# An eighth pair of attention chunks shares its weights, two copies and a read change engine, and some tiles move by 128 bytes

## The chip, the cores and the metric

The kernel runs on one core of a Trainium2 chip. The metric is the device time of one execution in microseconds (us). The engines are TensorE (PE, with its weight loads as PEld), VectorE (DVE), ScalarE (ACT), GpSimd (POOL) and SyncE (SP, which here only issues transfers).

## The reference

Two stages. The first is an attention without softmax over 8 batches of 2496 rows, whose weights are the squared positive part of the scaled scores and whose result is multiplied by `u`. The second is a mixture of experts on the 19968 rows that come out.

```python
scores = (1.0 / S) * (z @ z.T)          # z: 2496 x 64 in each batch
attn = np.maximum(scores, 0.0) ** 2
x = u * (attn @ v)                      # u, v: 2496 x 256

do_compute = x @ w_skip > 0             # rows that go to an expert
logits = x @ w_gate                     # 8 experts
e = argmax(logits); gate = softmax(logits)[e]
out = x + gate * (relu(x @ w1[e]) @ w2[e])   # 256 -> 1024 -> 256
```

The scores of a batch are symmetric: the weights of keys A for queries B are those of keys B for queries A, transposed.

## The kernel before

**Chunks and steps.** The queries of a batch are cut into five chunks, c0 to c4 (four of 512 rows, c4 of 448). The keys are cut into ten pairs of 128-row blocks, p = 0 to 9, and keys p belong to the rows of chunk p // 2. A chunk is ten steps, one for each p, in the order of the table `ORDER` (the first chunk of the first batch goes 0 to 9), so the attention has 400 steps. In a step, PE does 24 matmuls into the four accumulators of the chunk (`attend`, 18 where p = 9): first 12 for the half d = 0 of the 256 columns, then 12 for d = 1. The accumulators of a half are called `acc[0]` and `acc[1]` (two row groups of PE, of 64 rows each, work side by side, each into its own), and the sum of both is the result.

**Weights.** The weights of a step are made two steps ahead (`stage(s + 2)`, called ahead of the step's own matmuls). `weights` has two ways. A plain tile is computed: six score matmuls on PE (`scores`, L251) into one of two PSUM buffers, Relu (L290) and Square (L291) on ACT. A recalled tile comes from DRAM (`recall`, L280, issued three steps earlier still). Then both are split into a high part `ah` (L310, on ACT or DVE by `on_act`) and a rest `al` (L314, DVE).

**Pairs.** For each pair (A, B) in `PAIRS` chunk A keeps its weights for the keys of B: DVE transposes them (`keep`, L268, two of each tile), SP writes them to DRAM, and chunk B, later in the same batch, recalls the two tiles for the keys of A and computes no scores for them. Batch 0 has no pairs with chunk 0. `EXTRA` names plain tiles whose `ah` is cast on ACT, beside all tiles of pairs.

**End of a chunk.** After its last step (`finish`), each accumulator is read from PSUM: `part(d, 1)` copies `acc[1]` of half d to SBUF (L366), `part(d, 0)` adds `acc[0]` to it (DVE, L368). Then come a product with `u` (L371), transposes of the rows (L375) and stores. In emission order `part(0, ...)` comes between the two halves of the last step, `part(1, ...)` after the second. The next chunk's accumulators take the same four PSUM buffers, in the order in which the pool gets them back.

**Routing.** After every second chunk the list `after` sets, by steps after the chunk's end, the logits' matmuls (`gates`, L406, +2), their transposes from PSUM (`logits`, L428 to L432, +3), the routing on DVE (+4), the gate's Exp (+5) and `place` (+6), which counts tokens by matmuls with a triangle and with ones (L476) and reads the counts from PSUM on DVE (L480, L482). Both PSUM tiles, named `psm`, take one of the two buffers that the scores use.

**Experts.** From about 1330 us on, 40 units of up to three 128-token tiles run through the 8 experts: `unit` multiplies the turned tokens `xt` with the first weights (L593) and the hidden values with the second (L612). `xt` shares its buffers with `rt` of the attention. The tile `shift` (L527) is used by nothing; it moves the tiles that are allocated behind it.

**Order.** Each engine works through its own list in program order: an instruction that waits holds up all behind it on that engine.

Of the kernel before, what the change touches and what calls it, by code (L numbers as in the profile page):

```python
# [8 lines left out]
F32 = mybir.dt.float32  # L9
# [4 lines left out]
ALU = mybir.AluOpType  # L14
AX = mybir.AxisListType
PSUM = bass.MemoryType.PSUM

P = 128
# [7 lines left out]

PAIRS = ((0, 1), (0, 2), (1, 2), (1, 3), (2, 3), (2, 4), (3, 4))
ORDER = (  # L30
# [5 lines left out]
)  # L36
EXTRA = ((8,), (3, 8), (4, 5), (1,), ())


C_TRI, C_REV, C_OFF, C_IDS, C_THR, C_END = 0, 128, 192, 256, 260, 270  # L40
# [2 lines left out]
def f32(ap):  # L43
    return ap.bitcast(F32)
# [3 lines left out]
def attn_moe(ctx, tc, zT, uT, v, wg, w1, w2, cst, pad, out):  # L48
# [4 lines left out]
    nc = tc.nc  # L53
# [5 lines left out]
    E = w1.shape[0]  # L59
# [15 lines left out]
    rp = ctx.enter_context(tc.tile_pool(name="rp", bufs=2))  # L75
    gp = ctx.enter_context(tc.tile_pool(name="gp", bufs=1))
    op = ctx.enter_context(tc.tile_pool(name="op", bufs=2))
# [139 lines left out]
    def pairs(b):  # L217

        return PAIRS if b else [x for x in PAIRS if x[0]]

# [4 lines left out]
    def on_act(ci, p):  # L225
        b, c = ci // NQ, ci % NQ
        j = p // 2
        if (b, c) == (0, 0):
            return p in (4, 6)
        return (j, c) in pairs(b) or (c, j) in pairs(b) or p in EXTRA[c]  # L230

    kept = {x: dram.tile([QC, QC], F32, name="kept%d%d" % x) for x in PAIRS}
    HALF = (slice(0, 64), slice(64, 128))
# [109 lines left out]
    def spare(rows64=True):  # L343

        if rows64:
            return ps_s.tile([P, 2, QC], F32, name="psm", tag="s")
        return ps_acc.tile([P, 1, QC], F32, name="psm", tag="acc")
# [3 lines left out]
    def finish(ci):  # L351

        b, q0, n = chunks[ci]
        t0 = b * S + q0
        xT = xTs[ci] = uts.pop(ci)

        nm = n // 32
        xrow = xp.tile([P, QC // 32, D // 4], F32, name="xrow", tag="xrow")


        e = xrow.rearrange("p a b -> p (a b)").rearrange("p (d q) -> p d q", d=2)

        def part(d, t, acc):

            if t:
                (nc.scalar.copy if d else nc.vector.tensor_copy)(e[:, d, :n], acc[1][:, :n])  # L366
            else:
                nc.vector.tensor_add(e[:, d, :n], acc[0][:, :n], e[:, d, :n])  # L368

        def mul():  # L370
            nc.vector.tensor_mul(xT[:, :, :n], e[:, :, :n], xT[:, :, :n])  # L371

        def turn_rows(d):

            nc.vector.transpose(  # L375
                xrow[:, :nm, 32 * d : 32 * d + 32], xT[:, d, :n].rearrange("p (m i) -> p m i", i=32)
            )

        dsts = [xr, out]

        def store():
            dst = dsts.pop(0)
            for a in range(4):
                nc.sync.dma_start(
                    dst[t0 : t0 + n, 64 * a : 64 * a + 64].rearrange("(m i) e -> i m e", i=32),
                    xrow[32 * a : 32 * a + 32, :nm, :],
                )

        return part, mul, lambda: turn_rows(0), lambda: turn_rows(1), store

    def routing(cis, rows64=True):

        K = 4 * len(cis)
# [19 lines left out]
        pair = rp.tile([P, 8, 2], I32, name="pair", tag="pair", bufs=3)  # L413
        dest = rp.tile([P, 8], I32, name="dest", tag="dest", bufs=3)

        ex = rp.tile([P, 8, E], F32, name="ex", tag="ex")[:, :K, :]
        sm = rp.tile([P, 8, 1], F32, name="sm", tag="sm")[:, :K, :]
# [45 lines left out]
            nc.scalar.activation(ex, dls[0], AF.Exp)  # L463

        def place():
            nc.vector.tensor_reduce(sm, ex, axis=AX.X, op=ALU.add)
            nc.vector.tensor_scalar_add(sm, sm, 1e-9)
            nc.vector.reciprocal(f32(pair[:, :K, 1:2]), sm)
            ps = spare(rows64)
            hot_, pre_ = (x.rearrange("p t e -> p (t e)") for x in (hot, pre))  # L470
            ds_ = rp.tile([P, 8, E], F32, name="ds_", tag="ds_")[:, :K, :]
            df = rp.tile([P, 8], F32, name="df", tag="df")[:, :K]
            halves = list(enumerate(HALF)) if rows64 else [(0, slice(0, P))]
            for w, x in ((tri, hot_), (ones, pre_)):
                for t, h in halves:
                    nc.tensor.matmul(  # L476
                        ps[:, t, : K * E], w[h, :], x[h, :], start=(w is tri), stop=(w is ones)
                    )
            c = ps[:, :, : K * E].rearrange("p k (t e) -> p k t e", e=E)
            nc.vector.tensor_add(ds_, c[:, 0], eoff[:, :K, :])  # L480
            if rows64:
                nc.vector.tensor_add(ds_, c[:, 1], ds_)  # L482
            nc.vector.tensor_mul(ds_, ds_, hot)
            nc.vector.tensor_reduce(df, ds_, axis=AX.X, op=ALU.add)
            put_sums.append(df)
# [3 lines left out]
        def put_in(t0, t1):  # L489
# [4 lines left out]
            for t in range(t0, t1):  # L494
# [10 lines left out]
                puts.append(put)  # L505

        return gates, logits, route, counts, gate, place, put_in

    def count(name, rows64=True):
# [14 lines left out]
        for k in range(n):  # L524
            xgs[t].append(zp.tile([P, 2, D], F32, name="xg" + t, tag="z" + "hl"[k % 2], bufs=ZBUFS))

    gp.tile([P, 40], F32, name="shift")  # L527
    xtf, xts = [], [[], []]

    def x_tiles():  # L530
# [139 lines left out]
    def stage(s):  # L670
        if s < len(steps):
            aa[s] = weights(*steps[s], old.pop(s, None))
            return aa[s][2:]
        return lambda: None, lambda: None

    def put_some():

        for _ in range(4):
            if puts and puts[0][0] < step[0] - 1:
                _, dst, src = puts.pop(0)  # L680
                nc.sync.dma_start(dst, src)

    def ahead(s):
        if s < len(steps):
            ci, p = steps[s]
            if (p // 2, ci % NQ) in pairs(ci // NQ):
                old[s] = recall(ci, p)
                known.add(s)
# [62 lines left out]
    for s, (ci, p) in enumerate(steps):  # L751
        b, q0, n = chunks[ci]
        k = s % NP
        step[0] = s
        ahead(s + LA + 3)
        high, low = stage(s + LA)
        if k == 0:
            accs[ci] = [[ps_acc.tile([P, QC], F32, name="acc", tag="acc") for _ in range(2)] for _ in range(2)]
        ah, al = aa.pop(s)[:2]
        if k < NP - 1:  # L760
            high()
            low()
            for d in range(2):
                attend(b, n, p, d, accs[ci][d], ah, al, k == 0, False)
        else:
            part, mul, rows0, rows1, store = finish(ci)
            acc = accs.pop(ci)
            if s + LA in known:

                high()  # L770
                low()
                high = low = lambda: None
            for d in range(2):
                attend(b, n, p, d, acc[d], ah, al, False, True)
                part(d, 1, acc[d])
                if d:
                    high()
                part(d, 0, acc[d])
            low()
            mul()  # L780

            new.append(ci)
            if ci < NC - 1:
                after = [(rows0, 2), (rows1, 3), (store, 4), (store, 5)]
                if ci % 2 == 0:
                    gates, logits, route, counts, gate, place, put_in = routing(new)
                    after = [(gates, 2), (rows0, 2), (logits, 3), (rows1, 3), (route, 4), (counts, 4),
                             (store, 4), (gate, 5), (store, 5), (place, 6)]
                    for t in range(0, 4 * len(new), 2):
                        f = lambda put_in=put_in, t=t: put_in(t, t + 2)  # L790
                        if s + 6 + t < len(steps):
                            after.append((f, 6 + t))
                        else:
                            left.append(f)
                    new = []
                for f, k in after:
                    todo.setdefault(s + k, []).append(f)
            else:
                gates, logits, route, counts, gate, place, put_in = routing(new, False)
        for f in todo.pop(s, []):  # L800
            f()
        put_some()
# [55 lines left out]
    for e in range(E):  # L858
# [3 lines left out]
        for i in range(NFIX):  # L862
# [24 lines left out]
            if i == NFIX - 1:  # L887

                add(fills, (5, lambda: turn_pe(pair(e, NFIX + 1), turned(e, NFIX), 1, 2 * P)))
                n = nc.values_load(fin["arm"][0:1, e : e + 1], min_val=0, max_val=narms - 1)  # L890
# [6 lines left out]
        for arm in tc.Switch(n, narms, hint="rest%d" % e):  # L897
# [9 lines left out]
            for j, w in enumerate(ws):  # L907
                i = NFIX + j
                fills = {}
                after = ws[j + 1 :]  # L910
# [73 lines left out]
```

## Time and profile before

| what | value |
|---|---|
| median of three runs | 1842.22 us (1838.9 to 1843.4) |
| the profiled execution | 1840.9 us |
| its span | 1839.1 us |
| PE busy over the span | 1797.2 us (98%) |
| DVE, ACT busy | 1226.3 us (67%), 1117.7 us (61%) |
| attention | about 0 to 1330 us |
| experts | about 1330 to 1839 us |

The busy times say which engine is the bound; where an engine sat idle, and whose work ended that, is read from the waits and the timelines of the places in question.

### The profile page before, as it was taken

Reading aid. Unit: us, or ns where it says so; the run is one execution under the profiler, and the core shown is the slowest. Engines: PE = TensorE matmul, PEld = TensorE weight load, DVE = VectorE, ACT = ScalarE, POOL = GpSimd, SP = SyncE. Lnnn points to the kernel's source line nnn. Section 1 sums busy time; section 2 is a strip of 40 time slices with the busy share of each in tenths; the row PEclk is TensorE's granted clock in tenths of the full one; section 3 lists DMA queues with packets and bytes.
Section 4 is the critical chain, followed back from the end, with each engine's and each line's share of the span. In section 5 each row is a group of like instructions: output and inputs, shape, how many; then the busy total and the mean of one; then the engine's idle time right before and its main releaser. Section 6 shows DMA issues by size and latency. Waiting matters only on the chain. (4 is left out here: it accounts for less than half of the span.)

```text
span 1839.1 us, 40432 instructions
## 1 busy us (share of the span) xinstructions
PE 1797.2 (98%) x15928; PEld 1616.5 (88%) x15928; DVE 1226.3 (67%) x2169; ACT 1117.7 (61%) x1414; POOL 433.4 (24%) x429
## 2 busy tenths in 40 slices
PE   8999999999999999999999999999899999999998
PEld 6888888978888898788999888888799999999998
DVE  7777787877877787788778777868653343334432
ACT  8876776777677677767776776777433223323321
POOL 0001101210120220111022011112254556535621
PEclk9999999999999999999999999999999999999999
DMA  5574587477648746874683686468452233313210
GB/s 184 127 190 126 134 212 181 106 182 184 156 113 202 190 104 166 202 174 115 166 206 96 162 224 154 106 174 197 118 118 67 78 96 106 83 51 101 82 40 26
DMA packets 384501, 252.77 MB, mean 137 GB/s; under 512 B 204515, under 2 KB 318437, under 8 KB 384176
## 3 DMA queue, kind: packets, MB, share of 16 engines
q1 hardware_dynamic: 370176, 225.79, 49.5%
q0 software_dynamic: 13712, 22.99, 4.5%
q8 instruction: 141, 2.31, 0.5%
q14 instruction: 184, 1.51, 0.3%
q10 hardware_dynamic: 288, 0.17, 0.0%
HBM read 138.46 MB, written 111.05 MB: 136 GB/s over the span
## 5 line engine op out<-in xcount | busy, mean ns | idle before, releaser
L338 PE MATMUL acc<-ah,vh 64*128 64x512 f32 (+1 forms) x3120 | 722.5, 386 | 9.6 <-DVE xrow L366 4.9
L338 PE MATMUL acc<-ah,vl 64*128 64x512 f32 (+1 forms) x3120 | 707.1, 384 | 0.0
L314 DVE TENSOR_TENSOR al<-r,ah 128x1024 fp32r<-128x1024 f32 (+3 forms) x464 | 478.9, 1048 | 191.5 <-ACT ah L310 179.4
L338 PE MATMUL acc<-al,vh 64*128 64x512 f32 (+1 forms) x3120 | 554.8, 384 | 0.1
L338 PEld LDWEIGHTS acc<-ah,vh 64*128 64x128 f32 x3120 | 418.2, 184 | 64.9 <-DVE xrow L368 11.7
L338 PEld LDWEIGHTS acc<-ah,vl 64*128 64x128 f32 x3120 | 418.0, 185 | 38.7
L290 ACT ACTIVATE r<-ps 128x1024 f32<-128x1024 f32 (+1 forms) x292 | 294.8, 1010 | 255.7 <-PE ps L251 224.2
L495 POOL DMA_INDIRECT lst<-pair,dest x160 | 184.5, 1153 | 1105.4 <-DVE dest L493 1006.1
L338 PEld LDWEIGHTS acc<-al,vh 64*128 64x128 f32 x3120 | 363.0, 184 | 41.8 <-DVE al L314 2.6
L310 ACT CAST ah<-r 128x1024 fp32r<-128x1024 f32 (+1 forms) x329 | 277.0, 871 | 59.9 <-DMA r<-kept 34.7
L291 ACT ACTIVATE r<-r 128x1024 f32<-128x1024 f32 (+1 forms) x292 | 304.8, 1044 | 9.2
L598 ACT ACTIVATE hh<-psh 128x512 fp32r<-128x512 f32 (+1 forms) x172 | 99.0, 584 | 299.7 <-PE psh L593 259.8
L612 PE MATMUL y<-w2t,hh 128*128 128x256 f32 x1328 | 246.3, 286 | 0.4 <-ACT hh L598 0.4
L593 PE MATMUL psh<-xt,w1h 128*128 128x256 f32 (+1 forms) x1280 | 235.3, 284 | 1.9 <-ACT xt L566 1.5
L612 PEld LDWEIGHTS y<-w2t,hh 128*128 128x128 f32 x1328 | 208.2, 192 | 0.7 <-ACT hh L598 0.7
L599 DVE SCALAR_TENSOR_TENSOR hl<-psh,hh 128x512 fp32r<-128x512 f32 (+1 forms) x172 | 113.3, 671 | 136.4 <-ACT hh L598 131.2
L593 PEld LDWEIGHTS psh<-xt,w1h 128*128 128x128 f32 x1280 | 197.3, 188 | 3.0 <-issue 2.5
L612 PE MATMUL y<-w2t,hl 128*128 128x256 f32 x664 | 188.7, 284 | 0.3 <-DVE hl L599 0.2
L593 PE MATMUL psh<-xt,w1l 128*128 128x256 f32 (+1 forms) x640 | 181.1, 283 | 0.0
L251 PE MATMUL ps<-zh 64*128 64x512 f32 (+1 forms) x584 | 144.8, 407 | 14.4 <-ACT zh L108 4.6
L251 PE MATMUL ps<-zl,zh 64*128 64x512 f32 (+1 forms) x584 | 140.4, 391 | 0.0
L268 DVE STREAM_TRANSPOSE rt<-r 128x512 f32<-128x512 f32 x216 | 140.2, 687 | 0.0
(170 smaller groups left out, 1703.9 us busy)
## 6 DMA issues: line engine op xcount, KB each, us to landing
kept<-rt SPq DMA_DIRECT2D x216, 256.0 KB, 5.2
r<-kept SPq DMA_DIRECT2D x432, 128.0 KB, 3.9
raw<-in_v SPq DMA_DIRECT2D x80, 256.0 KB, 3.7
ut<-in_uT SPq DMA_DIRECT2D x32, 512.0 KB, 5.2
xr<-xrow SPq DMA_DIRECT2D x128, 128.0 KB, 3.2
out<-xrow SPq DMA_DIRECT2D x128, 128.0 KB, 3.2
raw<-in_w SPq DMA_DIRECT2D x64, 256.0 KB, 3.6
zf<-in_zT SPq DMA_DIRECT2D x40, 256.0 KB, 3.7
```

What stands on the lines that cost most here:

```text
L251: nc.tensor.matmul(to, k[h, o : o + P], queries(q, h, n), start=(m == 0), stop=(m == 2))
L268: nc.vector.transpose(t[:, :, 32 * k : 32 * k + 32], r[:, x, :].rearrange("p (m i) -> p m i", i=32))
L290: nc.scalar.activation(r[:, :, :n], ps[:, :, :n], AF.Relu, scale=isc)
L291: nc.scalar.activation(r[:, :, :n], r[:, :, :n], AF.Square)
L310: (nc.scalar.copy if on_act(ci, p) else nc.vector.tensor_copy)(h_, r_)
L314: nc.vector.tensor_sub(l_, r_, f32(h_))
L338: nc.tensor.matmul(acc[t][:, :n], w[h, x, dd], a[h, x, :n], start=(first and t not in halves[:m]), stop=(last and t not in halves[m + 1 :]),)
L495: put = nc.gpsimd.indirect_dma_start(out=lst, out_offset=bass.IndirectOffsetOnAxis(ap=dest[:, t : t + 1], axis=0), in_=pair[:, t, :], in_o ...
L593: nc.tensor.matmul(ps[:, j * W : (j + 1) * W], wt[:, a, o : o + P], x[:, d, :W], start=(m == 0), stop=(m == 5),)
L598: nc.scalar.activation(hh[:, : G * W], ps[:, : G * W], AF.Relu)
L599: nc.vector.scalar_tensor_tensor(hl[:, : G * W], ps[:, : G * W], 0.0, f32(hh[:, : G * W]), op0=ALU.max, op1=ALU.subtract)
L612: nc.tensor.matmul(ys[t], h[:, tt], w2t[f][:, k, :], start=(f == 0 and m == 0 and t % 2 == 0), stop=(f == NF - 1 and m == 2), skip_group_c ...
```

## The change

1. The pair (0, 3) joins `PAIRS`: in batches 1 to 7 chunk 0 keeps its tiles for the keys 6 and 7 too, and chunk 3 recalls its tiles for the keys 0 and 1.
2. `ORDER` gets other rows for c0 to c3; `EXTRA` puts the casts of c3's p = 6 and 7 (plain tiles) and of c4's p = 1 and 3 on ACT.
3. The copy of half 0's `acc[1]` at a chunk's end moves from DVE to ACT, where that of half 1 already is.
4. `place` copies the counts from PSUM to a new SBUF tile `c` on ACT, and DVE reads them there; the sum and reciprocal of the gate come after the copy in the program.
5. `logits` comes two steps after the chunk's end, not three, behind `gates` and ahead of `rows0`.
6. `shift` shrinks from 40 to 8 floats. With `c` (512 bytes) ahead of them, the tiles behind it end up at other offsets: `xt` from 206240 and 214432 to 206624 and 214816, so that their address within 512 bytes goes from 416 to 288.

```diff
-PAIRS = ((0, 1), (0, 2), (1, 2), (1, 3), (2, 3), (2, 4), (3, 4))
+PAIRS = ((0, 1), (0, 2), (0, 3), (1, 2), (1, 3), (2, 3), (2, 4), (3, 4))
 ORDER = (
-    (0, 1, 6, 2, 3, 7, 4, 8, 5, 9),
-    (2, 0, 3, 1, 4, 5, 8, 6, 7, 9),
-    (0, 4, 1, 6, 2, 7, 3, 8, 9, 5),
-    (2, 0, 3, 1, 8, 4, 9, 5, 6, 7),
+    (0, 1, 2, 3, 8, 4, 5, 6, 7, 9),
+    (2, 3, 0, 4, 1, 5, 8, 6, 7, 9),
+    (4, 0, 1, 6, 2, 7, 3, 8, 9, 5),
+    (6, 0, 2, 1, 8, 3, 9, 4, 5, 7),
     (0, 1, 2, 3, 4, 5, 6, 7, 8, 9),
 )
-EXTRA = ((8,), (3, 8), (4, 5), (1,), ())
+EXTRA = ((8,), (3, 8), (4, 5), (6, 7), (1, 3))
...
             if t:
-                (nc.scalar.copy if d else nc.vector.tensor_copy)(e[:, d, :n], acc[1][:, :n])
+                nc.scalar.copy(e[:, d, :n], acc[1][:, :n])
...
         def place():
-            nc.vector.tensor_reduce(sm, ex, axis=AX.X, op=ALU.add)
-            nc.vector.tensor_scalar_add(sm, sm, 1e-9)
-            nc.vector.reciprocal(f32(pair[:, :K, 1:2]), sm)
             ps = spare(rows64)
...
-            c = ps[:, :, : K * E].rearrange("p k (t e) -> p k t e", e=E)
+
+            c = rp.tile([P, 2, 8, E], F32, name="c", tag="c", bufs=1)[:, : len(halves), :K, :]
+            nc.scalar.copy(c.rearrange("p k t e -> p k (t e)"), ps[:, : len(halves), : K * E])
+            nc.vector.tensor_reduce(sm, ex, axis=AX.X, op=ALU.add)
+            nc.vector.tensor_scalar_add(sm, sm, 1e-9)
+            nc.vector.reciprocal(f32(pair[:, :K, 1:2]), sm)
             nc.vector.tensor_add(ds_, c[:, 0], eoff[:, :K, :])
...
-    gp.tile([P, 40], F32, name="shift")
+    gp.tile([P, 8], F32, name="shift")
...
-                    after = [(gates, 2), (rows0, 2), (logits, 3), (rows1, 3), (route, 4), (counts, 4),
+                    after = [(gates, 2), (logits, 2), (rows0, 2), (rows1, 3), (route, 4), (counts, 4),
                              (store, 4), (gate, 5), (store, 5), (place, 6)]
```

The first place is ACT's list around the end of c0 in batch 5. Before:

```order
L290 ACTIVATE r<-ps 128x1024
L291 ACTIVATE r<-r 128x1024
L310 CAST ah<-r 128x1024
L366 COPY xrow<-acc 128x512
L290 ACTIVATE r<-ps 128x1024
L291 ACTIVATE r<-r 128x1024
```

In the changed kernel the same place reads:

```order
L290 ACTIVATE r<-ps 128x1024
L291 ACTIVATE r<-r 128x1024
L290 ACTIVATE r<-ps 128x1024
L291 ACTIVATE r<-r 128x1024
L366 COPY xrow<-acc 128x512 x2
L310 CAST ah<-r 128x1024 x2
```

One copy has become two, and right ahead of them stands the Relu and Square of c1's second step, which is now a plain tile, where the cast of a recalled one stood.

The second place is DVE's list at the `place` of one pair of chunks (`ds_`, `df` and `dest` are the slots in the experts' lists). Before:

```order
L314 TENSOR_TENSOR al<-r,ah 128x1024
L466 TENSOR_REDUCE sm<-ex 128x8
L467 TENSOR_SCALAR sm<-sm 128x8
L468 RECIPROCAL pair<-sm 128x8
L480 TENSOR_TENSOR ds__7403<-psm,cs 128x64
L482 TENSOR_TENSOR ds__7403<-psm,ds__7403 128x64
L483 TENSOR_TENSOR ds__7403<-ds__7403,hot 128x64
```

In the changed kernel:

```order
L479 TENSOR_REDUCE sm<-ex 128x8
L480 TENSOR_SCALAR sm<-sm 128x8
L481 RECIPROCAL pair<-sm 128x8
L482 TENSOR_TENSOR ds__7418<-c,cs 128x64
L484 TENSOR_TENSOR ds__7418<-c,ds__7418 128x64
L485 TENSOR_TENSOR ds__7418<-ds__7418,hot 128x64
```

DVE's own order is the same; what it reads is now `c` and not `psm`. The reader of `psm` is on ACT's list, between the cast of one tile and the Relu of the next:

```order
L463 ACTIVATE ex<-dl 128x64
L290 ACTIVATE r<-ps 128x1024
L291 ACTIVATE r<-r 128x1024
L310 CAST ah<-r 128x1024
L478 COPY c<-psm 128x128
L290 ACTIVATE r<-ps 128x1024
```

The copy of the counts is the only instruction that has been added there.

One thing does not show in these lists. In the program as built, the second accumulator that a new chunk writes (`acc[1]` of half 0) stands in the PSUM buffer of the old chunk's half 0 `acc[0]` before the change (released by the add L368; at the end of c0 it is that of half 1's `acc[1]`, released by ACT's copy). After the change it stands at every boundary in the buffer of the old chunk's half 1 `acc[1]`, released by ACT's second copy. The first accumulator stands in the buffer of half 0's `acc[1]` before and after.

## Rows read from the trace of the kernel before

**Rows 1.** Window of the attention: length; PE, PEld, DVE, ACT, POOL busy; clock, DMA share, GB/s.

```profile
0.00:1330.00 1330.00, 1301.79 (x11825) 1123.34 (x11826) 1027.51 (x1775) 963.79 (x1108) 185.29 (x175) 1.00 0.65 161
```

**Rows 2.** Waits of PE's matmuls: total us, times, longest.

```profile
PE acc L338 <- DVE xrow L366: 4.9, 7, 1.3
...
PE acc L338 <- DVE xrow L368: 3.5, 14, 0.6
...
PE ps L251 <- DVE ds__6468 L482: 1.8, 1, 1.8
...
PE ps L251 <- DVE lg L428: 1.1, 3, 0.4
PE ps L251 <- DVE lg L432: 0.9, 4, 0.2
...
PE ps L251 <- DVE ds__18482 L482: 0.2, 1, 0.2
```

**Rows 3.** Timeline, end of c0 in batch 5: start, length, instruction [idle before].

```profile
866.71 0.41 PE L251 MATMUL ps<-zh 64*128 64x512 f32 x2
...
866.93 0.59 ACT L366 COPY xrow<-acc 128x512 f32<-128x512 f32 x1 [1.44 <-DMA ut<-in_uT]
...
867.18 0.42 PE L251 MATMUL ps<-zh,zl 64*128 64x512 f32 x2
867.36 0.68 DVE L366 COPY xrow<-acc 128x512 f32<-128x512 f32 x1
...
868.10 0.51 PE L338 MATMUL acc<-ah,vh 64*128 64x512 f32 x2 [0.50 <-DVE xrow L366]
...
868.44 0.39 PE L338 MATMUL acc<-ah,vl 64*128 64x512 f32 x2
```

**Rows 4.** The same view for PE's weight loads.

```profile
PEld acc L338 <- DVE xrow L368: 11.7, 23, 0.9
...
PEld acc L338 <- DVE xrow L366: 9.7, 14, 1.7
```

**Rows 5.** Timeline at a place in batch 2.

```profile
461.43 0.39 PE L338 MATMUL acc<-al,vh 64*128 64x512 f32 x2
...
463.59 0.50 PE L251 MATMUL ps<-zh 64*128 64x512 f32 x2 [1.77 <-DVE ds__6468 L482]
```

**Rows 6.** A group of the page: count, busy us, mean ns, idle before.

```profile
L268 DVE STREAM_TRANSPOSE rt<-r 128x512 f32<-128x512 f32 x216 | 140.2, 687 | 0.0
```

**Rows 7.** Timeline at the end of batch 4 (c4 to c0).

```profile
828.29 0.40 PE L251 MATMUL ps<-zh 64*128 64x512 f32 x2
...
829.20 1.03 ACT L290 ACTIVATE r<-ps 128x1024 f32<-128x1024 f32 x1 [0.50 <-PE ps L251]
...
831.23 0.52 ACT L366 COPY xrow<-acc 128x448 f32<-128x448 f32 x1
831.29 0.40 PE L251 MATMUL ps<-zh,zl 64*128 64x512 f32 x2
```

**Rows 8.** ACT's groups in the attention: count, busy us, mean ns, idle before.

```profile
L291 ACT ACTIVATE r<-r 128x1024 f32<-128x1024 f32 x244 | 259.0, 1062 | 7.7
...
L310 ACT CAST ah<-r 128x1024 fp32r<-128x1024 f32 x233 | 241.4, 1050 | 36.5 <-DMA r<-kept 27.9 <-PE acc L338 2.0 <-DVE ut L371 1.2
...
L366 ACT COPY xrow<-acc 128x512 f32<-128x512 f32 x32 | 18.8, 588 | 18.5 <-PE acc L338 11.8 <-DMA r<-kept 4.3 <-DMA ut<-in_uT 2.2
```

**Rows 9.** Timeline of two experts' units: first matmuls, each row a run.

```profile
1432.82 0.39 PE L593 MATMUL psh<-xt,w1h 128*128 128x256 f32 x2
...
1437.58 0.39 PE L593 MATMUL psh<-xt,w1h 128*128 128x256 f32 x2
...
1444.52 0.40 PE L593 MATMUL psh<-xt,w1h 128*128 128x256 f32 x2
...
1449.47 0.40 PE L593 MATMUL psh<-xt,w1h 128*128 128x256 f32 x2
```

**Rows 10.** Waits of ACT: total us, times, longest.

```profile
ACT ah L310 <- DMA r<-kept: 34.7, 25, 2.2
```

## The prediction

> **What bounds the kernel now.** I read the page's busy times first: PE is busy for 1797.2 of 1839.1 us. The window over the attention says that this holds there too: 1301.8 of 1330 us, with the granted clock at 1.00, the upper of its two levels (2.4 GHz) [rows 1]. DVE and ACT are busy for 77% and 72% of the attention, the transfers for 65%. So a part of the change is worth only what it takes from PE: matmuls that vanish, or idle time of PE that vanishes or appears. Next I read what PE waited for. Three kinds of waits recur in the attention [rows 2]: the accumulators at a chunk's end (L366 and L368, 21 waits, 8.4 us), the counts of `place` (L482, six waits from 1.8 down to 0.2; the four not shown are 1.8, 1.8, 1.5 and 0.6, 7.7 us together) and the turned logits (L428 and L432, 7 waits, 2.0 us). Last come the timelines of one place and of two chunk ends, to see what stands ahead of the late instruction. I cost the change against the profiled execution, 1840.9 us, which lies 1.3 us under the median of 1842.2.
>
> **How much a wait really costs.** The idle time printed with a matmul is less than what PE lost. In the timeline of a chunk end [rows 3] the pairs of matmuls start every 0.23 us (866.71, then 867.18 two pairs later), so the pair after 867.18 was due at 867.41. It came at 868.10, 0.69 late, and the next one came after 0.34 and not 0.23, another 0.11: 0.80 us for a printed 0.50, 0.3 more. The weight loads count 37 such waits (23 and 14) with 21.4 us [rows 4], which is an upper bound, since they run ahead of the matmuls. With 0.3 for each of the 37 on top of the matmuls' 8.4, the chunk ends cost 19.5 us now, between bounds of 8.4 and 21.4. At a `place` the next pair was due at 461.43 + 0.23 = 461.66 and came at 463.59 [rows 5]: 1.93, next to a printed 1.77, so I add 0.2 for each of the six and get 8.9. For the logits I add 0.3 for each of seven: 4.1 (at least 2.0).
>
> **Part 1, scores that vanish.** In seven batches chunk 3 recalls two tiles more, so 14 tiles of scores go. A tile is three pairs of matmuls, 3 x 0.23 = 0.70 us [rows 3]. All of it is on PE's path: -9.8 us. What replaces it lies beside PE: 28 more transposes on DVE at 0.687 us (19 us) [rows 6], against 40 copies that leave DVE (below); 14 fewer pairs of Relu and Square on ACT (2.1 us each, -29 us) [rows 7, 8]. The transfers of 28 writes and 56 reads more ride on queues whose share is 0.65 [rows 1]. I cost them at nothing for PE, as long as the recalled tiles land in time (rival 2).
>
> **Part 2, the place.** The PSUM tile of the counts is released today by DVE's second read, which stands behind an `al` and three small operations in DVE's list. Afterwards ACT reads it, right behind the cast that is due in that step, and by the built program the next scores go to the other of the two buffers in every batch; the buffer of the counts is wanted only one step, over 2.7 us, later. One small copy on ACT (a quarter of a microsecond by the size of the Exp there; 20 of them, 5 us on an engine with 28% to spare) is over by then. -8.9 us; if half of the places still waited, -4.
>
> **Part 3, logits a step sooner.** DVE reads the other PSUM tile a step earlier, so PE's next use of that buffer finds it free: up to -4.1, at least -2.0, unless the transposes queue behind DVE's `al`. The early call puts 0.4 us on DVE ahead of `rows0`, whose store is two steps off. I take -4, the value with the restarts in it.
>
> **Part 4, the chunk ends.** Here the change costs. Both accumulators of a new chunk's half 0 now wait for copies on ACT, and the second of these can only start when the old chunk's last matmul is done; DVE's copy, which could run beside the second half of the last step, is gone. What a boundary costs is then fixed by four durations: the copy began 0.22 us after the last matmul's slot (866.71 to 866.93), lasts 0.59, PE went on 0.06 after a copy's end (867.36 + 0.68 to 868.10), and the restart takes 0.11 [rows 3]: 0.98 us. The scores of the tile two steps ahead come between and cover 0.70 of it where that tile is plain; before the change they cover the same time at c0 to c1. But ACT works in order, and a Relu, a Square or a cast queued ahead of the copies makes them later. Boundary by boundary, with the tile types of the new `ORDER`:
> - c4 to c0 (c0's second and third tile plain): today ACT's copy stands at 831.23, behind the Relu from 829.20 and the Square; the scores end at 831.29 + 0.23 = 831.52 [rows 7]. Then the first copy takes that place and the second ends 0.52 later, at 832.27; PE at 832.33 and 0.11: 0.92 us.
> - c0 to c1 (second plain, third recalled): from the start of the last step the scores take 0.70, the 18 matmuls 2.04, end 2.74. The Relu starts at 0.91 (828.29 to 829.20 [rows 7]), Relu and Square take 2.09, two copies 1.18 [rows 8]: 4.18, PE at 4.24 and 0.11: 1.61 us, with no scores to cover it.
> - c1 to c2 (both recalled): no scores in between, and the cast of a recalled tile (1.05 [rows 8]) ahead of the copies: between 0.98 and 0.98 + 0.59 = 1.57, where the first copy too waits till the end; I take 1.3.
> - c2 to c3 (both recalled, a last step of 24 matmuls): 0.98.
> - c3 to c4 (both plain, 24 matmuls): the Relu's chain is done by the time the step ends, and 0.60 to 0.70 of the 0.98 is covered: 0.3.
>
> A batch: 0.92 + 1.61 + 1.3 + 0.98 + 0.3 = 5.1. Eight batches, with one c4 to c0 less: 40 us, where 19.5 stand now: +20.5. The lower end is each boundary without ACT's queue, 0.28, 0.98, 0.98, 0.98 and 0.28 = 3.5, or 28 for all: +8.5, and if the copy's start lag and restart, which stand in both, are smaller than these rows say (0.1 each for 39), +4. The upper end sets today's cost at 8.4: +31.
>
> **Part 5, addresses and the casts of `EXTRA`.** The casts move 1.05 us from DVE's 0.68 to ACT where both have slack: nothing. The tiles moved by 128 bytes modulo 512 are read by the experts' first matmuls. The same instruction on the same clock runs at two paces in the trace: from 1432.82 to 1437.58 stand 14 triplets, 42 matmuls at 113.3 ns, and from 1444.52 to 1449.47 14 triplets at 117.9 [rows 9]. For the 1920 such matmuls the 4.6 ns are 8.8 us: a gain of up to 8.8 if all ran slow now and fast then, a loss of as much the other way round. Six of the 40 units run fast now, which cuts the gain to about 7.5 and the loss to 1.3; I widen the loss to 4, since the second matmuls read their operands from the same memory. No row says which offset is the fast one, and both units read tiles of the same offset, so I take 0. The Trainium skill (SBUF — State Buffer, section "SBUF: two separate sides") says that PE's ports wait for no other engine and that transfers cannot slow them; by that an offset would be worth 0 too, but the two paces [rows 9] show that something beside the clock moves the pace here.
>
> **The sum.** -9.8 - 8.9 - 4 + 20.5 = -2.2 us, and 1 us for recalled tiles that come late to a cast. That is 1840.9 - 1.2 = 1839.7 for an execution like the profiled one; with the 1.3 us to the median 1841.0. Two of the terms, the c1 to c2 ends and the restarts, were taken near their upper ends, so I round down to 1840 us: no change that could be told from noise.
>
> **Rival 1: the boundaries cost less than I think.** If ACT's queue is mostly empty when the last matmul ends (for: in the attention it has 28% to spare [rows 1]; today the boundaries also contain waits of up to 1.3 us [rows 2] in which DVE's copy stood behind `al` operations, at 867.36 in [rows 3], 0.65 after the last matmul of the step, and these go), part 4 is +4 to +8.5 and the sum -9.8 - 8.9 - 4 + 6 = -16.7: 1825.5 us by the median. Against: the Relu ahead of the copies is in the list at c0 and c1, and 2.09 us long.
>
> **Rival 2: recalled tiles come late at the boundaries; slower.** At c1 to c2 and c2 to c3 the cast of a recalled tile stands ahead of both copies on ACT. If the tile has not landed, ACT waits and with it the copies and PE. Today ACT waits so 25 times, 1.4 us on average, up to 2.2 [rows 10], of 108 recalled tiles (14 in each of seven batches and 10 in the first), and PE hardly feels it, since a step lies between. With a sixth more reads the place is 16 boundaries; it decides as soon as more than about five of them wait. Half of them late by 1.4 gives +11: 1851 us; all of them +22.
>
> **Rival 3: the offset decides.** All units' first matmuls at the fast pace: some -7.5 from the sum, 1833; the loss: +4, 1844.
>
> **How the numbers follow.** The forecast, near 1840 (1834 to 1847), has 0.42; rival 1 0.25; rival 2 0.17; rival 3 0.09 for the fast pace and 0.07 for the slow one. The measurement of this kernel tells differences of about 0.3%, 5.5 us, from none, so that faster is below 1836.7 and slower above 1847.7. Faster: all of rival 1, the fast pace, and 0.10 of the forecast's own spread, 0.44. Slower: 0.13 of rival 2 and 0.04 of the others, 0.17. The same: 0.39. The range reaches from below rival 1 to rival 2 with half the boundaries late: 1823 to 1851. Of this the likeliest case alone fills 1834 to 1847.
>
> **What would show it.** Score matmuls fewer by 84, PE's waits on L482 and L428/L432 gone or under 1 us together; waits of the accumulators now on ACT's L366 and, by starts of pairs, 1.6 us at c0 to c1, about 1 at c2 to c3, 0.9 at c4 to c0. Rival 1 shows as such gaps under 0.5 us, rival 2 as casts waiting for r<-kept right ahead of the copies, rival 3 as another pace of the first matmuls in every unit. I am wrong outright if a new wait of PE appears inside the chunks, say on `al` in c0, where DVE now transposes three pairs.

## The result, and the profile after

The changed kernel takes 1847.9 us (median of 20 runs, 1844.1 to 1852.6) next to 1842.4 for the kernel before in the same comparison: a ratio of 1.0023 with an interval of 1.0014 to 1.0033. It is slower by some 4 us, where no change with a lean to a gain was forecast. The profiled execution of it (1852.6 us, span 1850.8) is at the upper end of its runs, so that its trace shows a little more loss than a usual execution has.

The waits of PE, in the same view as [rows 2] and [rows 4] (total us, times, longest):

```profile
PE acc L338 <- ACT xrow L366: 21.6, 22, 2.3
...
PE acc L338 <- DVE xrow L368: 0.2, 1, 0.2
```

```profile
PEld acc L338 <- ACT xrow L366: 46.9, 69, 2.7
```

The waits on `place` (L482) and on the logits (L428, L432) are gone from the list, as forecast. The waits at the chunk ends have moved from DVE to ACT, as forecast too, but they have grown from 8.4 to 21.8 us as printed. What PE really lost can be worked out from the starts of its matmuls: how far, against their pace of 0.227 us a pair, the new chunk's first pairs lag behind the last pairs of the old chunk (read at the fifth pair, which is still in the half d = 0). Summed over all batches, in us, with the forecast beside it:

| end | before | forecast | after |
|---|---|---|---|
| c4 to c0 (7) | 4.5 | 6.4 | 5.2 |
| c0 to c1 (8) | 7.8 | 12.9 | 9.7 |
| c1 to c2 (8) | 4.3 | 10.4 | 9.4 |
| c2 to c3 (8) | 2.9 | 7.8 | 19.8 |
| c3 to c4 (8) | 0.1 | 2.4 | 2.1 |
| all | 19.6 | 39.9 | 46.1 |

By this measure four of the five kinds came out under the forecast. One, c2 to c3, costs 2.5 us on average and not 0.98: 1.0 in batch 0, which has no pair (0, 3), 2.1 in batches 2, 4 and 6, and 2.7 to 3.5 in the other four. The table leaves out what PE loses later in the same step, where the accumulators of half 1 wait for DVE's adds (L368): 0.5 us in all before, 7.1 after, a part of it slow clock (below). Here is c2 to c3 in its longest form, in batch 3 (timeline, as in [rows 3]):

```profile
605.09 1.22 DVE L314 TENSOR_TENSOR al<-r,ah 128x1024 fp32r<-128x1024 f32 x1
...
606.40 1.03 ACT L290 ACTIVATE r<-ps 128x1024 f32<-128x1024 f32 x1 [2.33 <-DVE dest L495]
...
607.46 1.06 ACT L291 ACTIVATE r<-r 128x1024 f32<-128x1024 f32 x1
...
608.20 0.61 PE L338 MATMUL acc<-al,vh 64*128 64x512 f32 x4
608.55 1.99 ACT L310 CAST ah<-r 128x1024 fp32r<-128x1024 f32 x2
...
610.45 1.06 ACT L366 COPY xrow<-acc 128x512 f32<-128x512 f32 x2
...
611.08 1.28 PE L338 MATMUL acc<-ah,vh 64*128 64x512 f32 x2 [2.27 <-ACT xrow L366]
```

The slots of c2's last matmuls end at 608.65 (two pairs from 608.20 on). ACT's copies begin only at 610.45, behind two casts (that of tile 6, which `EXTRA` puts on ACT, and that of a recalled tile), behind a Square and behind a Relu that began at 606.40, after ACT had been idle for 2.33 us. A small DVE operation (L495) is printed as what ended that idle time; but the Relu reads no result of it. By the program the Relu waits for an `r` buffer to write into; the subtraction L314 right ahead of L495 (605.09 to 606.31), which reads the `r` of the tile before, ended 0.09 us before the Relu began. The kernel e10 below puts this to the test.

And there is a cost that stands in no wait. Windows of the same place (length; busy time of PE, PEld, DVE, ACT, POOL; clock; DMA share; GB/s):

```profile
600.00:608.50 8.50, 8.50 (x78) 6.87 (x74) 6.18 (x16) 6.08 (x7) 3.68 (x4) 1.00 1.04 266
608.50:611.00 2.50, 0.31 (x4) 0.00 (x0) 1.37 (x2) 2.47 (x5) 0.41 (x1) 0.95 0.98 250
611.00:618.00 7.00, 6.92 (x47) 5.64 (x49) 6.77 (x10) 3.03 (x5) 2.89 (x2) 0.77 0.92 231
618.00:628.00 10.00, 10.00 (x90) 8.87 (x88) 4.51 (x6) 6.54 (x7) 2.47 (x3) 1.00 0.45 108
```

After the pause PE is busy all the time, but with 47 matmuls in 7 us where it did 78 in 8.5: the granted clock is 0.77 over that window: the upper level (2.4 GHz) for a part of it and the lower one (1.2 GHz) for the rest. The same happens behind the pause at 942 us (clock 0.62 from 940 to 948) and behind that at 1275 (0.79 from 1275 to 1283); behind a fourth of about this length, at 281, the clock stays at 1.00. What the clock took is the missing share of each window: 0.23 of 7 us, 0.38 of 8 and 0.21 of 8, some 6 to 7 us in this execution.

### The profile page after: what moved, and what is told of

The parts are those of the page before. It is cut to its first block, busy times and chain, and to the rows that moved or that the text cites. A ratio compares the mean times of both kernels' runs of the same rounds, so it can differ in the third digit from the quotient of the medians.

```text
span 1850.8 us, 40455 instructions
## 1 busy us (share of the span) xinstructions
PE 1802.3 (97%) x15844; PEld 1594.5 (86%) x15844; DVE 1182.7 (64%) x2105; ACT 1157.0 (63%) x1499; POOL 440.9 (24%) x429
## 5 line engine op out<-in xcount | busy, mean ns | idle before, releaser
L338 PE MATMUL acc<-ah,vh 64*128 64x512 f32 (+1 forms) x3120 | 758.0, 390 | 24.1 <-ACT xrow L366 21.6
L338 PE MATMUL acc<-ah,vl 64*128 64x512 f32 (+1 forms) x3120 | 734.8, 387 | 0.0
L314 DVE TENSOR_TENSOR al<-r,ah 128x1024 fp32r<-128x1024 f32 (+3 forms) x464 | 479.5, 1049 | 259.1 <-ACT ah L310 247.7
L338 PE MATMUL acc<-al,vh 64*128 64x512 f32 (+1 forms) x3120 | 576.4, 385 | 0.0
L338 PEld LDWEIGHTS acc<-ah,vh 64*128 64x128 f32 x3120 | 455.9, 186 | 100.9 <-ACT xrow L366 46.9
L338 PEld LDWEIGHTS acc<-ah,vl 64*128 64x128 f32 x3120 | 455.0, 186 | 43.3
L290 ACT ACTIVATE r<-ps 128x1024 f32<-128x1024 f32 (+1 forms) x278 | 280.5, 1009 | 255.0 <-PE ps L251 210.1
L338 PEld LDWEIGHTS acc<-al,vh 64*128 64x128 f32 x3120 | 381.0, 185 | 47.6 <-DVE al L314 1.9
L310 ACT CAST ah<-r 128x1024 fp32r<-128x1024 f32 (+3 forms) x381 | 328.3, 891 | 40.0 <-PE acc L338 20.8
L291 ACT ACTIVATE r<-r 128x1024 f32<-128x1024 f32 (+1 forms) x278 | 289.9, 1043 | 8.8
L268 DVE STREAM_TRANSPOSE rt<-r 128x512 f32<-128x512 f32 x244 | 158.4, 688 | 1.3 <-DMA kept<-rt 1.2
```

The lines of the kernel that those rows point to most:

```text
L268: nc.vector.transpose(t[:, :, 32 * k : 32 * k + 32], r[:, x, :].rearrange("p (m i) -> p m i", i=32))
L290: nc.scalar.activation(r[:, :, :n], ps[:, :, :n], AF.Relu, scale=isc)
L291: nc.scalar.activation(r[:, :, :n], r[:, :, :n], AF.Square)
L310: (nc.scalar.copy if on_act(ci, p) else nc.vector.tensor_copy)(h_, r_)
L314: nc.vector.tensor_sub(l_, r_, f32(h_))
L338: nc.tensor.matmul(acc[t][:, :n], w[h, x, dd], a[h, x, :n], start=(first and t not in halves[:m]), stop=(last and t not in halves[m + 1 :]),)
```

## The experiments

Each kernel was timed in five rounds beside the kernel before on the same chip; the ratio is to that. Four theories came up, one after the other.

- **Theory A**: the ACT copies cost, because ACT's casts stand ahead of them.
- **Theory B**: the pair and the tables cost, whoever copies.
- **Theory C**: the types of the next chunk's first tiles set the end's price.
- **Theory D**: recalled tiles, which are asked for three steps ahead of their cast, hold the four `r` buffers, so that a plain tile's Relu or the next recall comes late; ACT's order carries that lateness to the copies.

In the table "all ends" and "c2 to c3" are read as in the table above, in one profiled execution of each kernel.

| kernel | ratio | interval | all ends, us | c2 to c3, us |
|---|---|---|---|---|
| the change | 1.0023 | 1.0014 to 1.0033 | 46.1 | 19.8 |
| e1_copy_dve | 1.0142 | 1.0126 to 1.0157 | 58.7 | 28.0 |
| e2_cast6_dve | 0.9998 | 0.9989 to 1.0008 | 37.1 | 10.9 |
| e3_before_addr | 0.9977 | 0.9966 to 0.9988 | 19.8 | 2.7 |
| e4_old_tables | 0.9973 | 0.9963 to 0.9982 | 30.8 | 6.7 |
| e5_place_logits | 0.9926 | 0.9913 to 0.9939 | 22.5 | 2.7 |
| e14_place_only | 0.9925 | 0.9912 to 0.9939 | 22.6 | 2.7 |
| e6_c3_order | 0.9986 | 0.9977 to 0.9995 | 45.4 | 18.4 |
| e7_mix | 0.9954 | 0.9939 to 0.9969 | 38.7 | 19.8 |
| e9_mix_act | 0.9940 | 0.9927 to 0.9953 | 29.3 | 10.6 |
| e10_c3_alternate | 0.9917 | 0.9903 to 0.9931 | 29.4 | 3.0 |
| e12_mix2_dve | 0.9856 | 0.9840 to 0.9872 | 21.2 | 2.3 |
| e13_mix2_act | 0.9874 | 0.9858 to 0.9891 | 25.5 | 6.3 |

**The copy back on DVE.** The changed kernel with

```diff
-                nc.scalar.copy(e[:, d, :n], acc[1][:, :n])
+                (nc.scalar.copy if d else nc.vector.tensor_copy)(e[:, d, :n], acc[1][:, :n])
```

> The changed kernel with one part undone: the copy of half 0's acc[1] at a chunk's end is on DVE again. Theory A (ACT's list at the chunk ends is what costs): the ends fall from 46 us to between 20 and 25, the long waits at c2 to c3 and the slow clock behind them go, and the time is near 1822 us (1817 to 1828). Theory B (the new pair and the order of steps cost, by recalled tiles that come late and by fuller ACT and DVE lists, whoever copies): DVE's copy stands as late behind its subtractions as ACT's behind its casts, and the time stays within 5 us of the changed kernel's 1848.

It was 1.2% slower than the change, not faster: theory A fell in this form. The timeline of c2 to c3 in batch 3 of this kernel shows both copies late, on two engines:

```profile
616.57 0.58 ACT L366 COPY xrow<-acc 128x512 f32<-128x512 f32 x1
...
617.20 0.49 PE L338 MATMUL acc<-ah,vh 64*128 64x512 f32 x1 [2.27 <-ACT xrow L366]
...
618.03 0.68 DVE L366 COPY xrow<-acc 128x512 f32<-128x512 f32 x1
...
618.76 0.50 PE L338 MATMUL acc<-ah,vh 64*128 64x512 f32 x1 [1.07 <-DVE xrow L366]
```

PE waits first for ACT's copy and, one matmul later, for DVE's, which stands behind two subtractions that waited for ACT's casts. So at this end the first accumulator stands in the buffer that ACT frees, and the second in the one that DVE frees; at c1 to c2 PE waits for both engines in the same order. With the new order of steps the copy on ACT is the better of two bad places, worth 22 us. The ends make 12.6 of it (58.7 against 46.1); besides, ahead of the last chunk ten stretches of 10 to 15 us ran at a mean granted clock of 0.66 to 0.83, where the change has three such places.

**One cast back on DVE.** The changed kernel with

```diff
-EXTRA = ((8,), (3, 8), (4, 5), (6, 7), (1, 3))
+EXTRA = ((8,), (3, 8), (4, 5), (7,), (1, 3))
```

> The changed kernel with only the cast of c3's first tile (p = 6) back on DVE; it stands on ACT's list ahead of the recalled tile's cast and both copies at c2 to c3. Theory A: that wait shrinks by the cast's 1.05 us in each of eight batches, 8 us, and the slow clock behind the longest ones (about 6 us in the profiled execution) goes too: 1834 us (1831 to 1840). Theory B: the cast was not what the copies waited for, but a recalled tile or a tile buffer; no change, 1845 to 1848.

0.25% (4.6 us) came back, less than theory A's 14 and more than theory B's nothing: c2 to c3 went from 19.8 to 10.9 us, and no stretch of slow clock is left ahead of the last chunk. The longest wait for a copy is now 1.2 us:

```profile
PE acc L338 <- ACT xrow L366: 13.7, 21, 1.2
...
PE acc L338 <- DVE xrow L368: 2.8, 9, 0.4
```

The second row shows one reason why no more came back: PE now waits nine times for DVE's adds, where the change has one such wait. In batches 2, 4 and 6, where neither kernel has slow clock, the new chunk starts 1.1 us sooner than in the change, and 0.8 of it is lost again in the second half of that step (1.1 us late there, next to 0.3). So the cast is one link of the chain that held the copies.

**The offset alone, and the old tables.** e3 is the kernel before with

```diff
-    gp.tile([P, 40], F32, name="shift")
+    gp.tile([P, 8], F32, name="shift")
```

> The kernel before with one part alone: the unused tile of 40 floats is 8 floats, so that the experts' token tiles move by 128 bytes to the same offset within 512 bytes as in the changed kernel. If the offset sets the pace of the experts' first matmuls, 34 of 40 units go from 117.9 to 113.7 ns a matmul and the time falls by 5 to 8 us, to 1834 to 1837. If it is something else that came with the change (the new tile, the other order), nothing moves: 1842.

It gains 0.23% (4.2 us), a little less than the 5 to 8 expected. In the traces of e3 and of the change nearly all units of two token tiles run their first matmuls at the pace that only six had before [rows 9]: 34 of 37 in both. A unit of the changed kernel, 14 triplets, 42 matmuls, in 4.76 us, 113.3 ns:

```profile
1397.43 0.39 PE L595 MATMUL psh<-xt,w1h 128*128 128x256 f32 x2
...
1402.19 0.39 PE L595 MATMUL psh<-xt,w1h 128*128 128x256 f32 x2
```

e4 is the changed kernel with `PAIRS`, `ORDER` and `EXTRA` of before.

> The changed kernel with the tables of before: pairs, order of steps and extra casts; the copies on ACT, the counts read by ACT, the earlier logits and the offset stay. Theory A: the ends stay dear, between 30 and 40 us, but without the cast of tile 6 ahead of the copies; the scores cost 9.8 us again: 1838 to 1848. Theory B: what the tables brought goes, the ends fall to about 20 us, and with the place, the logits and the offset gained the time is about 1822 (1818 to 1828).

1837.2 us (0.9973) lies at the edge of theory A's range and 9 us from theory B's. With the old tables the copies on ACT cost 30.8 us at the ends, so both theories hold a part: the new tables, scores saved and all, cost 9 us more than the old ones (1.0023 against 0.9973).

**Place and logits.** e5 is e3 with the place and the logits of the change; e14 is e5 with the logits at three steps.

> The kernel before with three parts of the change: the counts read by ACT, the logits a step sooner and the offset; the tables and the copy on DVE stay as before. If place and logits are worth what the waits of before say (13 us), it stands 13 us under the kernel with the offset alone (1838.3): 1825 us (1821 to 1829), with chunk ends of about 20 us. If the waits only move to the next user of those buffers: 1834 to 1838.

> The kernel e5 with the logits back at three steps, so that of the change only the counts read by ACT and the offset are in it. By the terms of the prediction the place is worth 8.9 us and the logits 4: it stands 4 us above e5 and about 9 us under the kernel with the offset alone, 0.9945 to 0.995 of the kernel before, with the waits of PE on the logits (about 2 us) back. If the two only share one wait, so that either alone takes it, it equals e5: 0.992 to 0.993.

e14 stands 0.52% under e3: the place read by ACT is worth 9.6 us (forecast 8.9). e5 and e14 are equal within 0.2%, though in e14 PE waits on the logits as it did in [rows 2]:

```profile
PE ps L251 <- DVE lg L428: 1.1, 3, 0.4
PE ps L251 <- DVE lg L432: 0.9, 4, 0.2
```

So the earlier logits bring nothing that these runs can show (their intervals leave room for 3 us either way). And e4 minus e5, 0.0047, is the price of the copy on ACT with the old order: 8.7 us (the intervals leave some 3 either way), with 8.3 us more at the ends.

**Two recalled tiles first.** The changed kernel with

```diff
-    (6, 0, 2, 1, 8, 3, 9, 4, 5, 7),
+    (2, 0, 6, 1, 8, 3, 9, 4, 5, 7),
```

> The changed kernel with only the order of c3 changed, to (2, 0, 6, 1, 8, 3, 9, 4, 5, 7): it starts with two recalled tiles, and its plain tile 6 comes third. Theory C (the ends are set by what stands in ACT's list ahead of the copies, and that is set by the types of the next chunk's first tiles): at c2 to c3 no Relu, Square and cast of tile 6 stand ahead of the copies, and its scores cover part of the wait; 20 us there become 3 to 8, the slow clock behind them goes: 1828 us (1823 to 1833). If recalled tiles that come late are the cause, two of them in a row are no better: 1842 or more.

A miss: c2 to c3 still costs 18.4 us. In this order no Relu stands ahead of the copies, so theory C as I put it is out. e7 takes the same order of c3, the old orders of c1 and c2, no extra casts in c3 and c4, and the copy on DVE; e9 is e7 with the copy on ACT.

> The pair (0, 3), place, logits and offset of the change, c0's new order, but c1 and c2 in the order of before, c3 as (2, 0, 6, 1, 8, 3, 9, 4, 5, 7), the extra casts of c3 and c4 on DVE and the copy of half 0 on DVE. Theory C: the ends cost about 20 us as before, and the scores' 9.8 us come on top of e5's gains: 1816 us (1812 to 1822). If the pair itself costs (its transposes, writes and recalled tiles), no better than e5: 1825 or more.

> The kernel e7 with one difference, the copy of half 0 on ACT as in the change. Theory C with the buffers as built (the second accumulator released by the copy after the last matmul at four ends of five): the ends cost 8 to 14 us more than in e7. If the ACT copy only costs behind casts: within 4 us of e7.

Here too c2 to c3 is dear, 19.8 and 10.6 us, and the trace of e7 says where it comes from (batch 2; SPq is SyncE's queue, which issues transfers):

```profile
425.04 3.69 SPq L683 DMA_DIRECT2D kept<-rt  x4
428.84 3.10 SPq L280 DMA_DIRECT2D r<-kept  x4
431.99 0.42 SPq L95 DMA_DIRECT2D raw<-in_v  x1
432.52 0.56 SPq L166 DMA_DIRECT2D ut<-in_uT  x1
433.18 1.94 SPq L280 DMA_DIRECT2D r<-kept  x4
...
435.30 1.04 ACT L310 CAST ah<-r 128x1024 fp32r<-128x1024 f32 x1 [3.62 <-DMA r<-kept]
436.25 0.58 ACT L366 COPY xrow<-acc 128x512 f32<-128x512 f32 x1
```

The recalled tile of c3's second step was asked for at 433.18, and ACT stood idle for 3.62 us ahead of its cast, with the copy behind. This is rival 2 of the prediction, in another order of steps than the change has. Theory D puts the late read down to a missing `r` buffer, as it does the late Relu in the change; for the read that is not shown. SP had issued transfers since 417.7 without a break of more than 0.4 us, and the read came right behind the others on its list. In e6 a read just as late (batch 6, 1102.96) came 0.36 us after the last subtraction was over and right behind the issue of `ut`. So the place in SP's queue explains these two late reads as well as a buffer does, or better. The e9 expectation missed too: the copy on ACT came out 0.14% faster, with overlapping intervals, and its ends cost 9.4 us less than e7's; in e7 DVE's copy stands behind the late tile's subtraction.

**Plain and recalled tiles in turn.** e10 is the changed kernel with one row:

```diff
-    (6, 0, 2, 1, 8, 3, 9, 4, 5, 7),
+    (6, 0, 8, 2, 1, 3, 9, 4, 5, 7),
```

> The changed kernel with only the order of c3 changed, to (6, 0, 8, 2, 1, 3, 9, 4, 5, 7): plain and recalled tiles alternate at its start. Theory D (recalled tiles hold the r buffers: with three recalled tiles in a row behind tile 6, its Relu gets the one buffer that is left, and waits for DVE's subtraction of the tile before; the Relu's lateness and not the number of ACT's casts makes the copies late): now two buffers are left for plain tiles, the Relu starts 1 to 2 us earlier, tile 8's scores cover 0.7, c2 to c3 falls from 20 us to 4 to 8 and the slow clock behind it goes: 1 to 1.3% under the changed kernel. Theory A alone (casts and copies queue on ACT): the list ahead of the copies is the same, only the 0.7 is covered: c2 to c3 12 to 15 us.

1826.3 us, 1.06% under the change. The same place in e10, batch 3:

```profile
598.58 1.03 ACT L290 ACTIVATE r<-ps 128x1024 f32<-128x1024 f32 x1 [0.61 <-DVE rt L268]
...
598.98 1.22 DVE L314 TENSOR_TENSOR al<-r,ah 128x1024 fp32r<-128x1024 f32 x1
...
600.73 2.01 ACT L310 CAST ah<-r 128x1024 fp32r<-128x1024 f32 x2
...
602.52 0.40 PE L251 MATMUL ps<-zh 64*128 64x512 f32 x2
...
602.64 1.06 ACT L366 COPY xrow<-acc 128x512 f32<-128x512 f32 x2
...
603.27 0.98 PE L338 MATMUL acc<-ah,vh 64*128 64x512 f32 x2
```

ACT's list ahead of the copies is operation for operation that of the change: Relu, Square, two casts, two copies. But the Relu starts 3.94 us ahead of the end of the old chunk's matmuls (602.52), not 2.25 (606.40 to 608.65), so that the first copy starts 0.12 after them and not 1.8. What the Relu no longer waits for can be read from the two timelines. DVE's list is the same in both up to here. In the change the Relu started 0.09 us after the subtraction of the tile before had ended (606.31); here it started 0.40 us before the same subtraction began (598.98). It is so in each of the seven batches with the pair (0, 3): in the change the Relu follows that subtraction, in e10 it does not wait for its end. That is what theory D says of the buffers, and neither ACT's own list, which is the same, nor the scores of tile 6, which end 4.7 us ahead of the old chunk's end in both, can explain it. c2 to c3 falls to 3.0 us, the scores of tile 8 cover 0.7 us at each end, and no slow clock follows. Theory A, which asked for 12 to 15 us, is out; theory D holds for the late Relu.

e12 and e13 do the same to e7 and e9 (c3 as 2, 6, 0, 8, 1, 3, 9, 4, 5, 7).

> The kernel e7 with the order of c3 changed to (2, 6, 0, 8, 1, 3, 9, 4, 5, 7). Theory D: in e7 the two recalled tiles at the start of c3 came late, since their reads wait for buffers and stand in one row on SP's queue; alternating, c2 to c3 falls from 20 us to 3 to 5, and with it goes the slow clock: 0.984 to 0.987 of the kernel before, below e5's 0.9926 by the scores' 9.8 us. If the pair's extra reads and writes themselves are what makes tiles late, c2 to c3 stays over 10 us and the time at e5's or above.

> The kernel e12 with the copy of half 0 on ACT as in the change. The ends cost about 8 us more than in e12 at c1 to c2, c3 to c4 and c2 to c3, and less at c0 to c1, where DVE's copy stands behind subtractions: within 0.4% of e12 either way; the better of the two says where the copy should be once the order is right.

e12, at 1816.0 us (0.9856), is the fastest kernel of the study: it has the pair, c0's order, the place, the earlier logits and the offset of the change, but keeps the copy and the extra casts of c3 and c4 on DVE, the old orders of c1 and c2, and lets recalled and plain tiles take turns at the start of c3. PE's waits at the ends are back at or under [rows 2]:

```profile
PE acc L338 <- DVE xrow L366: 3.4, 7, 0.9
PE acc L338 <- DVE xrow L368: 3.2, 14, 0.2
```

e13 has the copies on ACT and 4.3 us more at the ends: 6.2 less at c0 to c1 and c4 to c0 together, 10.5 more at the other three. The difference of the two, 0.18%, is within their intervals' reach. Against e5, e12 gains 0.70%, 12.9 us; the scores that the pair saves are 9.8 of it. So the pair itself, its transposes, writes and reads, costs PE nothing that these runs can show (the intervals leave some 4 us): that part of theory B is out. Its other part, that the order of steps costs whoever copies, was borne out by e1 and is what theory D explains.

## Why the prediction was wrong

The range held the time (1847.9 in 1823 to 1851), but the sign was missed: a ratio of 1.0023 is 4 us slower, where 2 us faster was forecast, and the cases of faster had the most weight. That the range held is partly luck: the offset gained 4.2 us that the sum had at 0. By its own steps:

- **Part 1, scores.** Right: 84 matmuls fewer (15844 in place of 15928), and nothing lost by the pair itself that the runs could show (e12 against e5).
- **Part 2, place.** Right in mechanism and size: 8.9 forecast, 9.6 measured (e14 against e3), and no wait on those counts is left.
- **Part 3, logits.** The waits went, the 4 us did not come: 0 within 3. The 0.3 us that I added for each of the seven waits was read from one chunk end and not from a wait on the logits.
- **Part 4, chunk ends.** The step that failed is the line "c2 to c3 (both recalled, a last step of 24 matmuls): 0.98". For c1 to c2 I let a cast ahead of the copies make them later, and at c4 to c0 and c0 to c1 I followed the Relu through ACT's list; for c2 to c3 I took the price of an empty ACT, although `EXTRA` had just put the cast of the chunk's first tile on ACT, ahead of the recalled one's. And I started every chain at the scores' end, as if a Relu needed nothing but its scores: it needs an `r` buffer too. It measured 2.5 us on average, 12 us more over eight batches. The other four kinds were 6 us cheaper than forecast. Nor did the sum have a term for the accumulators of half 1, at which PE lost 7.1 us where it had lost 0.5.
- **The clock.** No term for it stood in the sum, and no reason was given for leaving it out. Behind three of the four longest pauses at c2 to c3 a stretch at the lower clock level followed; some 6 to 7 us in the profiled execution. It goes with the pauses: e2 and e10 have no such stretch in the attention before its last chunk.
- **Part 5, offset.** The mechanism was seen and its sign left open, with 0 taken; it measured -4.2 us. Without it the change would have been 0.46% slower.

Rival 2 was nearer than the forecast: a tile's lateness is carried by ACT's order into the copies at c2 to c3. But in the change it is a plain tile that is late, for want of a buffer that the recalled ones hold, and not the recalled tile's transfer; that form came in e6 and e7. (Rival 2's "a sixth more reads" should be an eighth, 14 tiles on 108; nothing hung on it.) Rival 1 speaks of ACT's idle time, 28% of the attention; in the change ACT was idle for 2.33 us right ahead of the late Relu, so the idle time is of no use where an instruction that has to wait stands at the head of an engine's list.

Summed in ratios, in us of 1842: offset -4.2, place -9.6, logits 0, copy on ACT with the old order +8.7, and the tables on top of that +9.2, in which -9.8 of scores stand and so, by subtraction, about +19 of chunk ends and clock. Each term is the difference of one kernel to the next, so that they add up to the measured +4.2 by construction; the parts themselves are known to some 2 to 3 us each.

What stays open: how the 9.2 of the tables divides between the ends (15.3 us more in the traces than with the old tables) and the clock, since executions differ in how much slow clock they have. That the `r` buffers hold the Relu up was shown by another order of tiles, which also covers 0.7 us by scores; a fifth buffer, the direct test, was not tried. Whether the late reads of e6 and e7 come from the buffers or from SP's queue was not tested either; e12's order, which cures them, fits both.

## What to carry to other kernels

When a load is issued early, the buffer that it holds is taken from whoever shares the pool: count the buffers in flight at each step before putting several early loads in a row, and alternate them with work that frees buffers fast. Look too at what stands ahead of a load in the queue that issues it. An engine with idle time still delivers late when the head of its list waits; to price an instruction that moves to it, follow what is ahead of it back to its inputs and its output buffer, at every place where it will stand and not only at the ones with a familiar trace. And where the bounding engine pauses for more than a few short waits, look at its granted clock behind the pause: here the pause at 942 us, 2.3 us long, was followed by 8 us at a mean of 0.62, which took another 3.

## What the runs showed of the hardware

- The offset of a tile within 512 bytes changes the pace of matmuls that read it: 117.9 ns at 416, 113.3 to 114 at 288, for the same instruction at the same granted clock, in 30 of the 31 two-tile units that ran slowly before. The three units of three tiles (384 columns) went the other way, from 173.5 to between 175.6 and 177.9 ns a matmul. The Trainium skill (SBUF — State Buffer, section "SBUF: two separate sides") has it that PE's ports wait for no one; the runs show a difference with nothing but the offset changed (e3 against the kernel before, 0.9977). What in the memory makes it is not shown. Nor does the offset settle it alone: six units ran at the fast pace at 416, and three two-tile units ran at the slow one at 288, in e3 and in the change (two of those six among them each time). All of these are the first unit of all or the first behind the branch that chooses how many more units an expert gets; why is not explained.
- At c2 to c3 of the change, four pauses of PE are printed with 2.2 to 2.3 us of idle time. Behind three of them the granted clock fell: to a mean of 0.77 over 7 us, of 0.62 over 8 us and of 0.79 over 8 us. Behind the fourth, and behind the pauses of 1.3 us at the same place in batches 2, 4 and 6, it stayed at 1.00. The length of one pause does not settle it: in e6 (batch 2) two pauses of 0.9 us, at 442.7 and 444.1, were followed by a mean of 0.58 from 444 to 448.
